# A three-multiplication complex product rearranged, port sharing priced in the planner, z and Fourier steps issued earlier

## The chip, the cores and the metric

One core of a Trainium2 chip runs the whole program. The metric is the device time of one execution in microseconds (us); the kernel before takes 1736.83 us, the median of three runs (1736.76 to 1737.3).

## What is computed

The input x is 8 batches of 3072 rows by 256 columns, all fp32. The reference does this (setup left out):

```python
X = np.fft.rfft(x, axis=1)
Xr, Xi = X.real, X.imag
Yr = Xr @ w_r - Xi @ w_i + b_r
Yi = Xr @ w_i + Xi @ w_r + b_i
lam = 0.01
Yr = np.sign(Yr) * np.maximum(np.abs(Yr) - lam, 0.0)
Yi = np.sign(Yi) * np.maximum(np.abs(Yi) - lam, 0.0)
y = np.fft.irfft(Yr + 1j * Yi, n=3072, axis=1)
h = max(y @ w1, y @ w2, y @ w3)        # 256 -> 768, elementwise maximum
out = h @ w_out                        # 768 -> 256
```

The weights w1, w2, w3 and w_out arrive as float64 and are brought to pairs of fp16 numbers.

## The kernel before, in words

**Two parts that overlap.** The Fourier part (transform along the rows, complex weights, soft threshold, inverse transform) runs for one batch while the maxout part (three up products, maximum, down product) runs for the batch ahead of it. Nearly every product is made of three fp16 matmuls (`mm3`, L353 to L355): high times high, high times low, low times high. The first batch's Fourier part is fp32 and fills the first 100 us or so; batches 1 to 7 use the fp16 form.

**The maxout part.** A batch is four groups g of two column sets; a group has six slots f (768 = 6 x 128), and a batch has 48 half slots (`SLOTS`). In each slot `up` makes seven products into four PSUM banks pu, pw, pq, pv, which rotate over three buffers. pw gets one product, ScalarE copies it to SBUF (m5, which the trace calls m, L1132), then pw gets a second product. VectorE writes pq = pu + m (L1135), pq gets a product, ScalarE copies it into pv (L1145), and pq and pv get one each. VectorE makes h from them (L1150, twice), and `split` (L342, L343) makes the fp16 pair hh, from which `down` makes the output in pd.

**What feeds `up`.** Before each group, `load_z` reads two sets of z back from DRAM, `split_z` makes their fp16 pair (zh, zl), `inverse` makes y (pi, then yt), and `operands` makes four sums of the parts of y on GpSimd (ys, L1103, four instructions a group) and splits them to fp16 (yo, L342 and L343, on ScalarE and VectorE). In the before kernel `load_z` comes in slots f = 1 and 2, `split_z` in 2 and 3, `inverse` in 3 and 4, `operands` in 4.

**The Fourier part.** For each batch, eight quads go through `stage_a` (pa) to DRAM as a_d; then twelve steps k each load aj, split it (ah, al), make px (`stage_b`), split that (tt), multiply by the complex weights (`stage_w`), threshold, split (vp), rearrange through four DMAs (vq) and transform back (`stage_q`, pz) to z_d. Eleven steps of a batch are complex, one (k = 11) is plain. For a complex step the weights are applied with three real products: a common one, (Xr + Xi) times w_r, and two more, one added to it for each of the real and imaginary parts. `stage_w1` makes the common product in PSUM: the first matmul of the first half (L951) is 512 wide and writes it to both halves of the bank py, the other five (L955 to L957) are 256 wide and go to the first half; then ScalarE copies the first half over the second (L958). `stage_w2` adds the other two products on top, twelve matmuls. VectorE makes u = py times scale plus bias_c (L972), thresholds it in `soft_threshold` (L913, L914), and takes its largest magnitude (L994 in `finish_w`).

**What sets the order.** The kernel's instructions are first written in a program order: `run_until` runs each Fourier step when its position p in half slots comes. Then `gather`, `link` and `arrange` plan: they give each instruction a cost, find what it needs, and choose for each engine the order by a list schedule; PE's list looks at most 40 entries ahead, GpSimd's is kept as written. Only the order is kept: each engine then runs its instructions in that order and waits where something is late. In `gather` a VectorE instruction with two full-size inputs costs 0.07 us and 1.04 ns an element, a GpSimd instruction 0.1 us and 0.95 ns an element, and nothing says that the two can slow each other.

Of the kernel before, what the change touches and what calls it, by code (L numbers as in the profile page):

```python
# [101 lines left out]
MARGIN, AHEAD = 1.04, 3  # L102
# [13 lines left out]
class Op:  # L116
    def __init__(self, engine, label):
        self.engine, self.label, self.dma, self.busy, self.bytes = engine, label, False, 0.0, 0
        self.ins, self.reads, self.writes = [], {}, {}
# [15 lines left out]
def gather(traced, mark):  # L135
    ops, last, pinned = [], None, 0
    for n, i in enumerate(traced):
# [19 lines left out]
        else:  # L157
# [5 lines left out]
            else:  # L163
# [6 lines left out]
                else:  # L170
                    cost = 0.1 + n * 0.95e-3
# [66 lines left out]
def arrange(ops, pinned):  # L238
# [8 lines left out]
    ran = [False] * len(ops)  # L247

# [3 lines left out]
    while count < len(ops):  # L252
# [43 lines left out]
        else:  # L296
            free[e], issue[e], wait = t + o.busy, t, o.wait
# [15 lines left out]
def fourier_maxout_kernel(  # L313
# [24 lines left out]
    holds = []  # L338

# [31 lines left out]
    qf = const.tile([P, 2, P], F32, name="qf")  # L371
# [41 lines left out]
    def load_first_bias():  # L413
# [7 lines left out]
        nc.gpsimd.dma_start(out=qf, in_=mq[:, 0:2])  # L421
# [45 lines left out]
    def fft_limits(ws):  # L467
# [8 lines left out]
        split_scaled(*(t.rearrange("p a b -> p (a b)") for t in (qh, ql, qf)), Q_SCALE)  # L476
# [9 lines left out]
        )  # L486

# [180 lines left out]
    def batch(b, kind):  # L668
        if (b, kind) not in st:
            if kind in "az":  # L670
                st[b, kind] = dram.tile([N1, N2, D], F32, name=kind + "_d")
            else:
                w = NCH if kind == "x" else NJP if b else 2 * NJP
# [97 lines left out]

# [83 lines left out]
    def first_q(k):  # L855
# [3 lines left out]
        if k < NJP - 1:  # L859
            nc.tensor.matmul(pz, qf[:, 0], u.rearrange("p j d -> p (j d)"), start=True, stop=True)  # L860
        else:
            for j in range(2):
                nc.tensor.matmul(pv[:, j], qf[:, j], u[:, j], start=True, stop=True)
# [47 lines left out]
    def soft_threshold(k, u):  # L911
        t = fft.tile([P, 2, D], F32, name="t", bufs=1)
        nc.vector.tensor_scalar(out=t, in0=u, scalar1=-LAM, scalar2=LAM, op0=ALU.max, op1=ALU.min)  # L913
        nc.vector.tensor_tensor(out=u, in0=u, in1=t, op=ALU.subtract)  # L914
        st["u", k] = u

    def stage_w(k):
# [18 lines left out]
        u = fft.tile([P, 2, D], F32, name="u", bufs=2)  # L936
# [6 lines left out]
    def stage_w1(k):  # L943
# [15 lines left out]

    def stage_w2(k):  # L960
        if plain(k):
            return
        tt = st.pop(("t", k))
        py = st.pop(("py", k))
        for c, part, w in ((0, 1, 3), (1, 0, 2)):
            for h in range(KD):
                mm3(
                    py[:, c * D:(c + 1) * D], *(t[:, h, part * P:(part + 1) * P] for t in tt),
                    wch[:, h, w], wcl[:, h, w], start=False, stop=h == KD - 1, skip_group_check=True,
                )  # L970
        u = fft.tile([P, 2, D], F32, name="u", bufs=2)
# [6 lines left out]
    def finish_w(k):  # L978
# [13 lines left out]
        else:  # L992
            return
        st["max"] = nc.vector.tensor_reduce(  # L994
            out=batch(b, "u")[:, kb:kb + 1], in_=u.rearrange("p j d -> p (j d)"), axis=AX.X,
            op=ALU.max, apply_absolute_value=True,
        )
# [226 lines left out]
    for k in range(-3, NJP + 1):  # L1224
# [32 lines left out]
        if k == 6:  # L1257
            nc.sync.dma_start(out=ga_sb, in_=ga)
            load_bias()
# [28 lines left out]
    for b in range(NB):  # L1288
        for g in range(NCH // 2):
            nxt = (b, 2 * g + 2) if 2 * g + 2 < NCH else (b + 1, 0) if b + 1 < NB else None  # L1290
            first = b == g == 0
            halves, made = [], []
            for f in range(NF):
# [23 lines left out]
                if nxt and f in (2, 3):  # L1317
                    split_z(nxt[0])
# [47 lines left out]
```

## Time and profile before

| | |
|---|---|
| median of three runs | 1736.83 us |
| the profiled execution | 1739.03 us |
| its span, first to last instruction | 1737.2 us |
| busy: PE, VectorE, ScalarE, GpSimd | 97%, 75%, 69%, 10% |
| granted TensorE clock, mean over the span | 0.992 |
| chain that ended last: PE's share | 87% |

Of the span, the first 125 us or so are the loading, the fp32 batch and the preparation of the weights; the rest repeats the same 48 half slots eight times. A matmul of the trace lasts from its start to its modelled end, which lies behind the start of the next one, so a PE that is 97% busy says only that it is seldom empty. How much a matmul occupies PE is read from the distance of two starts. In the lists of groups, the columns are line, engine, operation, output <- input by the program's names, shapes, count, then busy us and mean ns of one, then idle us before it with what ended most of it.

### The profile page before, as it was taken

To read this page: it belongs to the slowest core of one execution; us is meant where nothing else is said; L and a number is where in the kernel's file an instruction comes from. 1 tells how busy PE (TensorE), PEld (TensorE's weight loads), DVE (VectorE), ACT (ScalarE), POOL (GpSimd) and SP (SyncE) were. 2 spreads that over 40 slices of the span, in tenths; PEclk is the share of its full clock that TensorE was granted. 3 is DMA by queue.
4 is the path that set the end of the run, shared out by engine and by line. 5 is a ranking of instruction groups with operands and counts; after the bars stand their busy time and mean duration, and the time that the engine had idled before them with its cause. 6 is when DMAs were issued, how large, how long until landed. Compare 5 with 4: busy or idle time off the path is not lost.

```text
span 1737.2 us, 38864 instructions
## 1 busy us (share of the span) xinstructions
PE 1684.9 (97%) x15509; PEld 1210.4 (70%) x15509; DVE 1295.3 (75%) x2241; ACT 1198.8 (69%) x2279; POOL 174.8 (10%) x200
## 2 busy tenths in 40 slices
PE   6989999999999999999999999999999999999998
PEld 3856767677676767767776777767777677776676
DVE  5988698678867878678886788768886697856542
ACT  2778687677766877577766777667776677656663
POOL 2000001111011111011111101111101111101110
PEclk8989999999999999999999999999999999999999
DMA  9645353434433433334333444333442233221111
GB/s 307 201 131 164 107 153 90 112 95 125 114 101 101 113 103 107 103 107 121 109 103 87 117 121 120 86 102 108 114 119 83 80 92 86 71 71 37 39 32 32
DMA packets 134996, 185.26 MB, mean 107 GB/s; under 512 B 17776, under 2 KB 113264, under 8 KB 134816
## 3 DMA queue, kind: packets, MB, share of 16 engines
q1 hardware_dynamic: 72784, 106.86, 22.9%
q10 hardware_dynamic: 61824, 75.52, 14.6%
q8 instruction: 122, 2.00, 0.5%
q14 instruction: 58, 0.48, 0.1%
q0 software_dynamic: 208, 0.39, 0.1%
HBM read 87.03 MB, written 75.50 MB: 94 GB/s over the span
## 4 chain that ended last, share of the span: by engine, by line
PE 87%; DVE 6%; ACT 3%; issue 2%; DMA 2%; ACTq 0%; SPq 0%; DVEq 0%
PE pd L353 9%; PE pd L354 9%; PE pd L355 9%; PE pq L353 4%; PE pw L353 4%; PE pw L355 3%; PE pw L354 3%; PE pq L355 3%; PE pq L354 3%; PE pu L353 3%; PE pu L355 3%; PE pu L354 3%; PE pa L756 3%; PE pi L1081 3%; PE py L353 2%; PE py L355 2%
## 5 line engine op out<-in xcount | busy, mean ns | idle before, releaser
L353 PE MATMUL pd<-woh,hh 128*128 128x256 f16 x1152 | 314.1, 273 | 0.6 <-ACT o L1174 0.6
L354 PE MATMUL pd<-wol,hh 128*128 128x256 f16 x1152 | 314.0, 273 | 0.0
L355 PE MATMUL pd<-woh,hh 128*128 128x256 f16 x1152 | 314.0, 273 | 0.0
L1150 DVE SCALAR_TENSOR_TENSOR h<-pq,c 128x384 f32<-128x384 f32 x192 | 106.8, 556 | 163.8 <-PE pq L355 133.5
L343 DVE TENSOR_TENSOR hh<-h,hh 128x768 f16<-128x768 f32 x192 | 189.4, 987 | 37.6 <-ACT hh L342 36.8
L355 PEld LDWEIGHTS <-wul 128*128 128x128 f16 x1344 | 131.3, 98 | 92.3 <-issue 5.5
L353 PEld LDWEIGHTS <-wuh 128*128 128x128 f16 x1344 | 131.3, 98 | 90.3 <-issue 28.4
L354 PEld LDWEIGHTS <-wuh 128*128 128x128 f16 x1344 | 131.4, 98 | 89.1 <-issue 33.6
L342 ACT ACTIVATE hh<-h 128x768 f16<-128x768 f32 x192 | 160.3, 838 | 37.1 <-DVE h L1150 33.0
L1103 POOL TENSOR_TENSOR ys<-yt 128x384 f32<-128x384 f32 x62 | 70.1, 1130 | 1114.2 <-ACT yt L1086 1114.2
L1132 ACT ACTIVATE m<-pw 128x384 f32<-128x384 f32 x192 | 93.8, 489 | 113.2 <-PE pw L355 107.9
L1135 DVE TENSOR_TENSOR pq<-pu,m 128x384 f32<-128x384 f32 x192 | 108.4, 565 | 75.8 <-ACT m L1132 74.4
L1138 ACT ACTIVATE r<-pw 128x384 f32<-128x384 f32 x192 | 94.0, 489 | 98.3 <-PE pw L355 87.9
L353 PE MATMUL pw<-yo,wuh 128*128 128x384 f16 x384 | 125.4, 326 | 12.6 <-ACT m L1132 8.1
L353 PE MATMUL pq<-yo,wuh 128*128 128x384 f16 x384 | 125.3, 326 | 8.1 <-DVE pq L1135 5.4
L354 PEld LDWEIGHTS <-hh 128*128 128x128 f16 x1152 | 112.7, 98 | 27.9 <-issue 0.8
L353 PEld LDWEIGHTS <-hh 128*128 128x128 f16 x1152 | 112.7, 98 | 27.6
L354 PE MATMUL pw<-yo,wuh 128*128 128x384 f16 x384 | 125.1, 326 | 2.4 <-DVE yo L343 2.4
L354 PE MATMUL pu<-yo,wuh 128*128 128x384 f16 x384 | 125.2, 326 | 1.9 <-DVE yo L343 1.9
L353 PE MATMUL pu<-yo,wuh 128*128 128x384 f16 x384 | 125.5, 327 | 0.0
L355 PE MATMUL pu<-yo,wul 128*128 128x384 f16 x384 | 125.2, 326 | 0.0
L355 PE MATMUL pw<-yo,wul 128*128 128x384 f16 x384 | 125.1, 326 | 0.0
(280 smaller groups left out, 4514.8 us busy)
## 6 DMA issues: line engine op xcount, KB each, us to landing
z_d<-zs ACTq DMA_DIRECT2D x96, 256.0 KB, 2.5
out_dram<-o ACTq DMA_DIRECT2D x192, 128.0 KB, 2.4
zq_c<-z_d SPq DMA_DIRECT2D x126, 192.0 KB, 3.4
aj<-a_d SPq DMA_DIRECT2D x90, 256.0 KB, 3.0
xq_c<-in_x_dram SPq DMA_DIRECT2D x112, 192.0 KB, 3.5
a_d<-aq ACTq DMA_DIRECT2D x112, 192.0 KB, 3.0
vq<-vp SPq DMA_DIRECT2D x308, 64.0 KB, 2.3
rw<-in_moe_w_dram SPq DMA_DIRECT2D x12, 384.0 KB, 7.2
```

Source lines behind the costliest of these rows:

```text
L342: nc.scalar.activation(out=hi, in_=src, func=AF.Copy)
L343: nc.vector.tensor_tensor(out=lo, in0=src, in1=h, op=ALU.subtract)
L353: nc.tensor.matmul(o, lh, rh, start=start, stop=False, **kw)
L354: nc.tensor.matmul(o, lh, rl, start=False, stop=False, **kw)
L355: nc.tensor.matmul(o, ll, rh, start=False, stop=stop, **kw)
L756: nc.tensor.matmul(pa[r][64 * c:64 * c + 64], fr[rows], xs[c][rows], start=True, stop=True)
L1081: nc.tensor.matmul(pi[p][:, o:o + N1], lz[r, n2, h * P:(h + 1) * P], ga_sb[r, lg, c * NQ + n2, :], start=lz is zh and lg == 0, stop=lz is zl,)
L1103: (nc.vector if first else nc.gpsimd).tensor_tensor(out=o, in0=x0, in1=x1, op=op)
L1132: nc.scalar.activation(out=m5, in_=pw, func=AF.Copy)
L1135: nc.vector.tensor_tensor(out=pq, in0=pu, in1=m5, op=ALU.add)
L1138: nc.scalar.activation(out=r1, in_=pw, func=AF.Relu, scale=-H_SCALE)
L1150: nc.vector.scalar_tensor_tensor(out=h32[:, n], in0=o, scalar=scale, in1=c, op0=ALU.mult, op1=ALU.max)
```

## The change

It has four parts. **One**: `stage_w1` makes the common product once, six 256-wide matmuls into the first half of the bank; VectorE adds it to bias_c, for both halves at once, into u in SBUF (L991 of the changed kernel), and ScalarE's copy is gone. `stage_w2` makes the other two products alone, and one accumulating instruction adds u, scales, and keeps the smallest value (L1006). `soft_threshold` becomes accumulating too (keeps the largest), so that the separate maximum of `finish_w` remains only for plain steps. As the bias is now added ahead of the scale, bias_c is loaded anew and divided by the scale on GpSimd once a batch, with three short VectorE instructions for the factor and three more in the preparation. **Two**: the planner knows that a GpSimd instruction and a VectorE instruction with two full-size SBUF inputs run at 0.54 of their speed while they overlap, and prices a two-input GpSimd instruction at 2.2 ns an element. **Three**: z is loaded, split and transformed one slot earlier in every group but the last of batch 0 (batches and groups are counted from 0). **Four**: the Fourier steps of batches 2 to 7 are written 2.5 half slots earlier. Besides, qf becomes two tiles in a buffer that is used later.

```diff
-MARGIN, AHEAD = 1.04, 3
+MARGIN, AHEAD, SHARED = 1.04, 3, 0.54
...
-                    cost = 0.1 + n * 0.95e-3
+                    cost = 0.1 + n * (0.95e-3 if not sizes[0] else 2.2e-3 if len(ends[0]) > 1 else 1.13e-3)
+                op.port = engine == "Pool" or engine == "DVE" and sum(
+                    z == n and place(a.bass_ap.tensor) != "PSUM" for z, a in zip(sizes[0], ends[0])
+                ) > 1
...
-            free[e], issue[e], wait = t + o.busy, t, o.wait
+            end, wait = t + o.busy, o.wait
+            if o.port:
+                other = "DVE" if e == "Pool" else "Pool"
+                j, until = beside.get(other, (k, 0.0))
+                if until > t:
+                    both = min(until - t, o.busy)
+                    until += both * (1 / SHARED - 1)
+                    end += both * (1 / SHARED - 1)
...
-    qf = const.tile([P, 2, P], F32, name="qf")
+    qf = [fft.tile([P, D], F16, name="qf", tag="ts", bufs=2).bitcast(F32) for _ in range(2)]
...
             st[b, "sx"] = power("s0x", e, -1.0, 261.0), power("s1x", e, 1.0, add)
-
+            t = small("six", U32, 2)
+            nc.vector.tensor_scalar(out=t, in0=e, scalar1=-1.0, scalar2=st["inv"], op0=ALU.mult, op1=ALU.add)
...
+            load_bias()
+            nc.gpsimd.tensor_scalar(
+                out=bias_c, in0=bias_c, scalar1=t.bitcast(F32), scalar2=1.0, op0=ALU.mult, op1=ALU.mult
+            )
...
     def soft_threshold(k, u):
...
-        nc.vector.tensor_tensor(out=u, in0=u, in1=t, op=ALU.subtract)
+        nc.vector.tensor_tensor_reduce(
+            out=u, in0=u, in1=t, scale=1.0, scalar=0.0, op0=ALU.subtract, op1=ALU.max,
+            accum_out=batch(b, "u")[:, NJP + kb:NJP + kb + 1],
+        )
...
     def stage_w1(k):
...
         for h in range(KD):
-            lh, ll = (t[:, h, 2 * P:3 * P] for t in tt)
-            rh, rl = (w[:, h, 0] for w in (wch, wcl))
-            if h == 0:
-                nc.tensor.matmul(
-                    pv, lh, wch[:, 0, 0:1].broadcast_to([P, 2, D]), start=True, stop=False
-                )
-            else:
-                nc.tensor.matmul(pv[:, 0], lh, rh, start=False, stop=False)
-            nc.tensor.matmul(pv[:, 0], lh, rl, start=False, stop=False)
-            nc.tensor.matmul(pv[:, 0], ll, rh, start=False, stop=h == KD - 1)
-        nc.scalar.activation(out=pv[:, 1], in_=pv[:, 0], func=AF.Copy)
+            mm3(
+                pv[:, 0], *(t[:, h, 2 * P:3 * P] for t in tt), wch[:, h, 0], wcl[:, h, 0],
+                start=h == 0, stop=h == KD - 1,
+            )
+        st["u", k] = u = fft.tile([P, 2, D], F32, name="u", bufs=UB)
+        nc.vector.tensor_tensor(out=u, in0=pv[:, 0:1].broadcast_to([P, 2, D]), in1=bias_c, op=ALU.add)
...
     def stage_w2(k):
...
-        for c, part, w in ((0, 1, 3), (1, 0, 2)):
+        for c, part, w in ((1, 0, 2), (0, 1, 3)):
...
-        u = fft.tile([P, 2, D], F32, name="u", bufs=2)
-        nc.vector.scalar_tensor_tensor(
-            out=u, in0=py.rearrange("p (c d) -> p c d", c=2), scalar=st[k // NJP, "sx"][1], in1=bias_c,
-            op0=ALU.mult, op1=ALU.add,
+        u = st.pop(("u", k))
+        nc.vector.tensor_tensor_reduce(
+            out=u, in0=py.rearrange("p (c d) -> p c d", c=2), in1=u, scale=st[b, "sx"][1], scalar=0.0,
+            op0=ALU.add, op1=ALU.min, accum_out=batch(b, "u")[:, kb:kb + 1],
         )
...
-            p = 9.8 + 1.85 * (k + 2) if b == 1 else (b - 1) * SLOTS + 2.5 * (k + 2)
+            p = 9.8 + 1.85 * (k + 2) if b == 1 else (b - 1) * SLOTS + 2.5 * (k + 1)
...
+            ahead = int(b > 0 or g < 3)
...
-                if nxt and f in (3, 4):
-                    halves.append(inverse(nxt[0], nxt[1] + f - 3))
-                if nxt and f == 4:
+                if nxt and f in (3 - ahead, 4 - ahead):
+                    halves.append(inverse(nxt[0], nxt[1] + f - 3 + ahead))
+                if nxt and f == 4 - ahead:
                     y_next = operands(*halves)
```

The planned orders show it at three places. The first is PE in batch 4, group 1, slot 1, where pw gets its two products. The names are tiles with their buffer numbers, and of each product of three matmuls only the last or the first row stands here; the weight loads between them are left out. Before:

```order
L355 MATMUL pu_14632<-yo_14325,wul_79 128x384
L353 MATMUL pw_14633<-yo_14328,wuh_78 128x384
L355 MATMUL pw_14633<-yo_14328,wul_79 128x384
L353 MATMUL pw_14633<-yo_14331,wuh_78 128x384
L355 MATMUL pw_14633<-yo_14331,wul_79 128x384
L353 MATMUL pd_14671<-woh_82,hh_13818 128x256
```

and now the same slot:

```order
L373 MATMUL pu_14697<-yo_14256,wul_80 128x384
L371 MATMUL pw_14698<-yo_14259,wuh_79 128x384
L373 MATMUL pw_14698<-yo_14259,wul_80 128x384
L371 MATMUL pd_14736<-woh_83,hh_13818 128x256
L373 MATMUL pd_14737<-woh_83,hh_13818 128x256
L371 MATMUL pw_14698<-yo_14262,wuh_79 128x384
L371 MATMUL pq_14707<-yo_14259,wuh_79 128x384
```

Before, pw's second product followed its first at once; now fifteen matmuls into pd stand between them.

The second place is VectorE where the operands of batch 3's first group are made (yo), beside the scales of a Fourier batch (ex, mv, s0v, s1v) and the h of a slot. Before:

```order
L774 TENSOR_SCALAR mv<-ex,addx,ebf 128x1
L777 TENSOR_SCALAR mv<-mv 128x1
L343 TENSOR_TENSOR yo<-yt,yo 128x768
L343 TENSOR_TENSOR yo<-ys,yo 128x768
L450 TENSOR_SCALAR s0v<-mv 128x1
L450 TENSOR_SCALAR s1v<-mv 128x1
L1150 SCALAR_TENSOR_TENSOR h_10625<-pq,c_10615 128x384
L1150 SCALAR_TENSOR_TENSOR h_10625<-pv,r_10607 128x384
L343 TENSOR_TENSOR yo<-yt,yo 128x384
```

and now:

```order
L361 TENSOR_TENSOR yo<-yt,yo 128x768
L1183 SCALAR_TENSOR_TENSOR h_10508<-pq,c_10498 128x384
L1183 SCALAR_TENSOR_TENSOR h_10508<-pv,r_10490 128x384
L361 TENSOR_TENSOR yo<-ys,yo 128x768
L361 TENSOR_TENSOR yo<-yt,yo 128x384
L460 TENSOR_REDUCE ex<-pt 128x1
L1168 TENSOR_TENSOR pq<-pu,m_10602 128x384
L361 TENSOR_TENSOR yo<-ys,yo 128x768
L461 TENSOR_SCALAR ex<-ex 128x1
```

The two h instructions stood behind two yo instructions, and now stand between them; the scales have moved behind all four.

The third place is PE at the 46th complex step of the program: the end of the common product, what follows it, and the first matmul of the other two. Before:

```order
L957 MATMUL py_14457<-wch_76,tt_14155 128x256
L353 MATMUL pq_14403<-yo_13660,wuh_78 128x384
L355 MATMUL pq_14403<-yo_13660,wul_79 128x384
L353 MATMUL pv_14418<-yo_13660,wuh_78 128x384
L353 MATMUL py_14457<-wch_76,tt_14155 128x256
```

and now, at the same step:

```order
L373 MATMUL py_14315<-wch_77,tt_14096 128x256
L371 MATMUL pu_14340<-yo_13568,wuh_79 128x384
L371 MATMUL pw_14341<-yo_13571,wuh_79 128x384
L371 MATMUL pd_14379<-woh_83,hh_13818 128x256
L371 MATMUL pd_14380<-woh_83,hh_13818 128x256
L371 MATMUL py_14315<-wch_77,tt_14096 128x256
```

Between the common product and the other two stood two products; now there are two and fifteen matmuls into pd.

## Rows read from the trace of the kernel before

**Rows 1.** The page, part 1: busy us, share of the span, instructions.

```profile
PE 1684.9 (97%) x15509; PEld 1210.4 (70%) x15509; DVE 1295.3 (75%) x2241; ACT 1198.8 (69%) x2279; POOL 174.8 (10%) x200
```

**Rows 2.** One stretch: us, then PE, PEld, DVE, ACT, POOL busy, PE clock, DMA.

```profile
1500.00:1600.00 100.00, 94.98 (x919) 68.59 (x918) 58.22 (x91) 61.62 (x114) 13.21 (x18) 1.00 0.21 56
```

**Rows 3.** Groups of instructions by line and shape: the complex step.

```profile
L972 DVE SCALAR_TENSOR_TENSOR u<-py,s1x,bias_c 128x512 f32<-128x512 f32 x77 | 57.4, 746 | 9.7 <-PE py L355 9.4
...
L994 DVE TENSOR_REDUCE mxu<-u 128x1 f32<-128x512 f32 x84 | 57.0, 679 | 0.4
...
L951 PE MATMUL py<-wch,tt 128*128 128x512 f16 x77 | 29.2, 379 | 1.0 <-ACT zs L1013 0.8
...
L958 ACT ACTIVATE py<-py 128x256 f32<-128x256 f32 x77 | 28.4, 368 | 13.5 <-PE py L957 11.5 <-DVE zl L348 0.5
...
L955 PE MATMUL py<-wch,tt 128*128 128x256 f16 x77 | 21.0, 273 | 0.0
...
L849 DVE CUSTOM_DVE_ANT_0 uf<-uf,t 128x512 f32<-128x512 f32 x12 | 8.3, 690 | 1.1 <-ACT uf L848 0.6
```

**Rows 4.** Who PE waited for: us in total, times, longest.

```profile
PE pw L353 <- ACT m L1132: 8.1, 14, 0.6
...
PE pq L353 <- DVE pq L1135: 5.4, 7, 1.2
...
PE pw L353 <- DVE h L1150: 4.1, 6, 0.8
PE pw L354 <- DVE yo L343: 2.4, 3, 1.0
PE pu L354 <- DVE yo L343: 1.9, 2, 1.2
...
PE py L353 <- ACT py L958: 0.2, 1, 0.2
```

**Rows 5.** PE in order of time: start, us, instruction; pw's two products.

```profile
1010.76 0.33 PE L354 MATMUL pw<-yo,wuh 128*128 128x384 f16 x1
1010.92 0.33 PE L355 MATMUL pw<-yo,wul 128*128 128x384 f16 x1
1011.83 0.32 PE L353 MATMUL pw<-yo,wuh 128*128 128x384 f16 x1 [0.58 <-ACT m L1132]
```

**Rows 6.** ScalarE's copies m (in order of time) and pv (its group).

```profile
1011.28 0.49 ACT L1132 ACTIVATE m<-pw 128x384 f32<-128x384 f32 x1 [0.46 <-PE pw L355]
...
L1145 ACT ACTIVATE pv<-pq 128x384 f32<-128x384 f32 x192 | 91.2, 475 | 25.2 <-PE pq L355 13.1 <-DMA z_d<-zs 2.4 <-PE pv L1123 0.9
```

**Rows 7.** VectorE in order of time, ahead of PE's longest wait for pq.

```profile
1399.60 0.95 DVE L343 TENSOR_TENSOR hh<-h,hh 128x768 f16<-128x768 f32 x1
...
1401.88 1.75 DVE L343 TENSOR_TENSOR hh<-h,hh 128x768 f16<-128x768 f32 x1
1403.56 1.75 DVE L343 TENSOR_TENSOR yo<-yt,yo 128x768 f16<-128x768 f32 x1
1405.23 0.55 DVE L1135 TENSOR_TENSOR pq<-pu,m 128x384 f32<-128x384 f32 x1
```

**Rows 8.** GpSimd in order of time: beside rows 7, and once beside an idle VectorE.

```profile
1402.78 1.71 POOL L1103 TENSOR_TENSOR ys<-yt 128x384 f32<-128x384 f32 x1
...
1560.66 0.99 POOL L1103 TENSOR_TENSOR ys<-yt 128x384 f32<-128x384 f32 x1 [47.04 <-ACT yt L1086]
```

**Rows 9.** DMA issues: KB each, median us from issue to landing.

```profile
aj<-a_d SPq DMA_DIRECT2D x90, 256.0 KB, 3.0
...
a_d<-aq ACTq DMA_DIRECT2D x112, 192.0 KB, 3.0
```

**Rows 10.** Groups by line and shape: a step's entry, aq, ah and al.

```profile
L348 DVE SCALAR_TENSOR_TENSOR al<-aj,s0x,ah 128x512 f16<-128x512 f32 x84 | 71.5, 852 | 9.1 <-ACT ah L347 8.8
...
L758 ACT ACTIVATE aq<-pa 112x512 f32<-112x512 f32 x112 | 64.5, 592 | 18.3 <-PE pa L756 17.4 <-ACT zs L1013 0.9
...
L347 ACT ACTIVATE ah<-aj,s0x 128x512 f16<-128x512 f32 x84 | 60.1, 717 | 1.0 <-ACT m L1132 0.7 <-ACT tt L347 0.2
```

More of the change, by code (lines that the diff above doesn't have):

```diff
@@ L118, in __init__ @@
         self.engine, self.label, self.dma, self.busy, self.bytes = engine, label, False, 0.0, 0
-        self.ins, self.reads, self.writes = [], {}, {}
+        self.ins, self.reads, self.writes, self.port = [], {}, {}, False
 def region(a):
@@ L247, in arrange @@
     ran = [False] * len(ops)
+    beside = {}
     def start(e, k):
@@ L296, in arrange @@
         else:
-            free[e], issue[e], wait = t + o.busy, t, o.wait
+            end, wait = t + o.busy, o.wait
[6 more added lines that the diff above has]
+                    end += both * (1 / SHARED - 1)
+                    for u in ops[j].users:
+                        ready[u] = max(ready[u], until + 0.1)
+                    free[other], beside[other] = max(free[other], until), (j, until)
+                    wait = end - t + 0.1
+                beside[e] = k, end
+            free[e] = end
         open_[e].remove(k)
@@ L420, in load_first_bias @@
         nc.gpsimd.dma_start(out=bias[64:65, 1, :], in_=rows[0])
-        nc.gpsimd.dma_start(out=qf, in_=mq[:, 0:2])
+        for j in range(2):
+            nc.gpsimd.dma_start(out=qf[j], in_=mq[:, j])
     def load_bias():
@@ L475, in fft_limits @@
         st["sc"] = power("sc", e, -1.0, 267.0, 1)
-        split_scaled(*(t.rearrange("p a b -> p (a b)") for t in (qh, ql, qf)), Q_SCALE)
+        for j in range(2):
+            split_scaled(qh[:, j], ql[:, j], qf[j], Q_SCALE)
         mb = small("mxb")
@@ L486, in fft_limits @@
         )
+        low, add = st["lim", "x"]
+        least, st["inv"] = small("leastx"), small("invx")
+        nc.vector.tensor_scalar(
+            out=least, in0=st["eb"], scalar1=add, scalar2=-62.0, op0=ALU.subtract, op1=ALU.add
+        )
+        nc.vector.tensor_scalar(out=low, in0=low, scalar1=least, scalar2=None, op0=ALU.max)
+        nc.vector.tensor_scalar(out=st["inv"], in0=add, scalar1=-1.0, scalar2=254.0, op0=ALU.mult, op1=ALU.add)
     def split_fft_weights(ws):
@@ L672, in batch @@
             else:
-                w = NCH if kind == "x" else NJP if b else 2 * NJP
+                w = NCH if kind == "x" else 2 * NJP
                 st[b, kind] = fft.tile([P, w], F32, name="mx" + kind + "0" * (b == 0), bufs=3 if b else 1)
@@ L859, in first_q @@
         if k < NJP - 1:
-            nc.tensor.matmul(pz, qf[:, 0], u.rearrange("p j d -> p (j d)"), start=True, stop=True)
+            nc.tensor.matmul(pz, qf[0], u.rearrange("p j d -> p (j d)"), start=True, stop=True)
         else:
             for j in range(2):
-                nc.tensor.matmul(pv[:, j], qf[:, j], u[:, j], start=True, stop=True)
+                nc.tensor.matmul(pv[:, j], qf[j], u[:, j], start=True, stop=True)
         return pv
@@ L991, in finish_w @@
             st["v", k] = [v[:, :, 0], v[:, :, 1]]
[L992 to L997, printed above, removed]
+            if plain(k):
+                nc.vector.tensor_reduce(
+                    out=batch(b, "u")[:, kb:kb + 1], in_=u.rearrange("p j d -> p (j d)"), axis=AX.X,
+                    op=ALU.max, apply_absolute_value=True,
+                )
     def stage_q(k):
@@ L1316, in fourier_maxout_kernel @@
                 run_until(b * SLOTS + (2 * g) * NF + 2 * f + 1)
-                if nxt and f in (2, 3):
+                if nxt and f in (2 - ahead, 3 - ahead):
                     split_z(nxt[0])
-                if nxt and f in (1, 2):
-                    load_z(nxt[0], nxt[1] + f - 1)
+                if nxt and f in (1 - ahead, 2 - ahead):
+                    load_z(nxt[0], nxt[1] + f - 1 + ahead)
             downs += [(1, *m) for m in made]
```

11 lines of the change are left out of this document (8 added, 3 removed).

## The prediction

> **What bounds the kernel now.** I read the busy shares first. PE is busy for 97% of the span, VectorE for 75%, ScalarE for 69% [rows 1]. A PE row lasts past the start of the next one, so I took start distances too: 384-wide matmuls start 0.16 us apart while each row is 0.33 us long [rows 5]. The program is therefore a queue of PE work with short gaps, and there are two ways to a shorter time: less PE work, or fewer gaps. Second came the list of whom PE waited for [rows 4]. After the opening no DMA is in it. Five entries carry the loss: ScalarE's copy m 14 times, VectorE's pq sum 7 times, h 6 times and yo 5 times. An entry shows less than PE loses, since the tail of the row before hides part: in rows 5 the idle is 0.58 us, but the starts are 0.91 us apart where 0.16 would do, 0.75 us lost. So I add 0.17 us to each wait. Third I read one wait of each kind in order of time, to see what it is made of.
>
> The waits for m are a matter of order. pw's second product comes straight behind its first, the copy m needs 0.49 us in between [rows 6], and with signalling PE loses 0.75 us [rows 5]. The waits for pq, h and yo are another matter. Ahead of the longest one VectorE's hh took 1.75 us, where one of the same shape had taken 0.95 us two rows earlier, and yo took 1.75 us as well [rows 7]; beside them GpSimd's ys took 1.71 us, where it takes 0.99 us with VectorE idle [rows 8]. The two engines slow each other, and the planner of the kernel before did not know it: 0.95 / 1.75 = 0.54 is the rate at which they run together. At the other waits for pq, h and yo that I looked at in the trace, ys is running or has just ended too. The stretch in which Fourier work has run out shows the most open PE, 5 us in 100 [rows 2].
>
> **The change, part by part.** The sum is made against the profiled execution, 1739.03 us; its span is 1737.2 us. The median of the runs is 1736.83 us, 2.2 us under the profiled execution, and I take the differences to that median.
>
> *PE work.* A complex step loses one 512-wide matmul and gets a 256-wide one in its place. The rows differ by 379 - 273 = 106 ns [rows 3], and there are 77 steps: **8.2 us less**. PE is the queue that everything stands in, so nearly all of it is on the path.
>
> *Second pw product.* I counted in both orders. The second product of pw follows the first with nothing between 13 times before and 6 times now; at 0.75 us [rows 5] that is 5.2 us. With exactly one 384-wide product between (0.49 us) there were 13 places and are 4; five of these lost a quarter microsecond, so about 1 us goes. **6 us less.** The bounds are 0, should PE only wait elsewhere, and 8.1 + 14 x 0.17 = 10.5 us, the whole entry [rows 4].
>
> *Second pq product.* It needs the copy of pq into pv, 475 ns [rows 6], as long as m. With one product of 0.49 us between, 0.75 - 0.49 = 0.26 us is lost by the same reckoning. There were 16 such places and there are 6 now: **2.6 us less**, bounds 0 and 16 x 0.26 = 4.2 us.
>
> *Waits beside GpSimd.* The entries for pq, h and yo are 5.4 + 4.1 + 2.4 + 1.9 = 13.8 us in 18 waits [rows 4], with 0.17 us each **16.9 us**. The new order knows the slowing. At the second place shown, h has moved ahead of the second yo. The yo waits were where the last inverse matmul stood 2.9 and 3.4 us of PE work before the first use of its result; now it is 8.5 us and 3.9 us. One of these two is cured; the other, in the group that is not fed earlier, hardly changes. I take two thirds of the whole, **11 us less**, because the planner still rates a few operations low; the bounds are 0 and 16.9.
>
> On how GpSimd and VectorE meet, the rows decide for sharing: in rows 7 and 8 both sides of a meeting are long at once, 1.75 against 1.71 us. The Trainium skill (SBUF — State Buffer, "SBUF: two separate sides") says instead that the pair of ports they share is an exclusive lock, so that one of the two runs at its full speed and the other is blocked for the whole instruction; here both slow down, so the trace does not agree. By that rule the planner's 0.54 would put the delays on the wrong instructions, and the sum would end some 11 us higher.
>
> *New waits.* (a) The product sum now goes through VectorE: PE may start the other two products only when u = py + bias_c has been read out of the bank. The trace has no such instruction. Nearest are 746 ns for a form with the same operands and a scale, and 690 ns for one without PSUM [rows 3]; I take 0.72 us. With 0.26 us of signalling (0.75 - 0.49, rows 5 and 6) it needs 0.98 us. The copy on ScalarE that it replaces took 368 ns [rows 3], PE waited for it once [rows 4], and the work between was mostly 0.98 us. Now 71 of the 77 steps have at least 1.3 us between, half of them 1.96 us or more, and six less than 1.2 us. Cost: 0 to 2 us, mostly where VectorE is late; I take 1 us. If the cover went, the next thing late would be PE itself. (b) VectorE loses 746 + 679 ns a complex step (the scaled sum, the separate maximum) and gets an add and one accumulating sum of about 0.72 + 0.69 us [rows 3], with two short reads of accumulators. That is even, and VectorE is not the bound. ScalarE loses 28 us of copies, off the path. (c) Three short instructions join the scales of a batch; these stand behind the four yo now, at worst half a microsecond a batch. GpSimd gets one instruction a batch between groups of ys, and SP two small loads, queued with 32 us or so of program order to spare. (d) The plain step's result is now wanted 4.5 to 5 us of PE work after its product in five batches, 7 us before; I allow 1 us in all.
>
> Sum: -8.2 - 6 - 2.6 - 11 + 1 + 1 = **-25.8 us**. That gives 1713.2 us for the profiled execution and 1711.0 us for the median; I forecast **1712 us**, as the last two terms are the least sure. The orders of the first 115 us are all but the same, so the waits there stay.
>
> **The rivals.**
>
> *The waits beside GpSimd stay (12%).* If whichever engine comes second is held for the whole of the other's instruction (up to the 0.99 us of ys), the planner's delays fall on the wrong instructions, and pq, h and yo come late at new places. For it: 0.95 + 0.99 = 1.94 us is not far from 1.75. Against: the twin lengths in rows 7 and 8. The 11 us are not gained: 1712 + 11 = 1723 us. (The Trainium skill's page named above states such a lock.)
>
> *The first step of a batch comes late (10%).* The Fourier steps stand 2.5 half slots earlier, so the first px of a batch follows the last pa of it after 15.0 us of PE work in batches 3 to 6, 24.1 before, and after 11.6 us in batch 2, 17.6 before. Between them lie two aq copies (1.18 us), the landings of a_d and aj (3.0 us each), ah and al (0.72 and 0.85 us): 8.8 us without issue and queueing [rows 9, 10]. If queueing makes it 17.5 us, six batches lose 2.5 us each: 1712 + 15 = 1727 us. Against: no PE wait of the steady part before is for a DMA.
>
> *Only the PE work counts (9%).* The gaps only move, because PE is held up by whatever VectorE and ScalarE can deliver: 1736.8 - 8.2 = 1728.6 us. Against: VectorE has a quarter of its time free [rows 1].
>
> *Slower: PE waits at the complex steps (5%).* Place: the first matmul of the other two products, behind u on VectorE; everything on PE queues behind it. If VectorE has just begun an instruction of 1.75 us [rows 7], u is ready after 1.75 + 0.98 = 2.7 us against a typical 1.96 us: 0.75 us lost. At all 77 steps that is 58 us, against a gain of 26 otherwise: 1737 + 32 = 1769 us. It decides when the mean wait passes 27 / 77 = 0.35 us. Against: GpSimd is busy for only 10% [rows 1], and pq, which waits on VectorE in the same way, was late 7 times in 192.
>
> *All the gaps go (4%).* Every bound at its better end: -8.2 - 10.5 - 4.2 - 16.9 = -39.8 us would need a perfect order; the six bare pw pairs alone forbid 4.5 us of it, so 1702 us.
>
> **How the numbers follow.** The forecast has 60%. Its own range is 1704 to 1720 us, from two thirds of 16.9 being anything from a third to all. The range of 8 in 10 takes in the first two rivals and most of the third: **1703 to 1728 us**. No change means within 0.2%, 3.5 us, about what a measurement of this kernel can tell. Faster than that end the forecast, the first, third and last rival and nearly all of the second: 0.91. Slower: the fourth rival, 0.05. Same: the rest, 0.04, the second and third in a worse size.
>
> **What would show it.** In the profile after: py has no 512-wide group, and its 256-wide rows are 273 ns; PE's wait for m falls to 6 or 7 times; the waits for pq, h and yo fall to under 6 us together, and hh and yo still take up to 1.75 us beside ys; PE's new wait for u is under 2 us. It is wrong if PE waits for u or for aj by more than 5 us, or if the entries of rows 4 keep their size under other lines.

## The result and the profile after

The change takes 1711.66 us (median of four runs, 1711.22 to 1713.43), and the kernel before on the same chip 1737.07 us (1736.76 to 1739.97). The ratio is 0.9848 with an interval of 0.9836 to 0.9861: **faster by 25.4 us**, 1.5%. The forecast was 1712 us. The profiled execution of the change took 1711.6 us, its span 1709.7 us.

The page of the changed kernel, parts 1 and 4 and four groups of part 5, against [rows 1, 3]:

```profile
PE 1671.7 (98%) x15509; PEld 1209.9 (71%) x15509; DVE 1285.1 (75%) x2427; ACT 1174.9 (69%) x2203; POOL 178.6 (10%) x208
...
PE 94%; DVE 2%; DMA 2%; ACT 1%; issue 1%; ACTq 0%; SPq 0%; DVEq 0%
...
L361 DVE TENSOR_TENSOR hh<-h,hh 128x768 f16<-128x768 f32 x192 | 193.9, 1012 | 30.5 <-ACT hh L360 30.4
...
L1136 POOL TENSOR_TENSOR ys<-yt 128x384 f32<-128x384 f32 x62 | 74.4, 1200 | 1044.6 <-ACT yt L1119 1044.6
...
L1165 ACT ACTIVATE m<-pw 128x384 f32<-128x384 f32 x192 | 94.1, 490 | 117.6 <-PE pw L373 115.7
...
L371 PE MATMUL py<-wch,tt 128*128 128x256 f16 x504 | 137.7, 273 | 0.6 <-DVE u L991 0.4
```

PE has the same number of instructions and 13 us less busy time. No group of 512-wide f16 matmuls into py is left; all are 256 wide at 273 ns. ys still takes 1.2 us in the mean where it takes 0.99 us beside an idle VectorE, so GpSimd and VectorE still meet; the busy shares of the other engines have not moved. What has moved is the list of whom PE waited for, which answers to [rows 4] (engine, tile and line, what it waited for, us in total, times, longest; idle times up to 0.15 us are not in it):

```profile
PE pw L371 <- ACT m L1165: 4.5, 10, 0.7
...
PE pz L371 <- DMA vq<-vp: 2.2, 1, 2.2
...
PE pu L372 <- DVE yo L361: 1.2, 1, 1.2
...
PE pq L371 <- ACT pv L1178: 0.7, 2, 0.4
PE pw L372 <- DVE yo L361: 0.6, 2, 0.4
...
PE py L371 <- DVE u L991: 0.4, 2, 0.2
...
PE pz L372 <- DVE vp L366: 0.3, 1, 0.3
```

The entries for pq and h on VectorE, 9.5 us before, are gone. Those for yo fell from 4.3 to 1.8 us, the one for m from 14 waits to 10. The new wait for u is 0.4 us. ScalarE, which before stood 18.8 us at yo for a late ys, now stands 1.4 us:

```profile
L360 ACT ACTIVATE yo<-ys 128x768 f16<-128x768 f32 x64 | 53.3, 833 | 1.8 <-POOL ys L1136 1.4 <-ACT pv L1178 0.2 <-ACT m L1165 0.2
```

Of the kernel before:

```profile
L342 ACT ACTIVATE yo<-ys 128x768 f16<-128x768 f32 x64 | 53.7, 838 | 18.8 <-POOL ys L1103 18.8
```

The stretch in which Fourier work has run out, 5 us open before [rows 2], is now 2 us open:

```profile
1500.00:1600.00 100.00, 97.98 (x930) 70.23 (x929) 54.64 (x86) 64.30 (x117) 10.08 (x8) 1.00 0.18 47
```

One entry is new and was in no step of the prediction: pz waited 2.2 us for the transfer of vq, once, in batch 1. VectorE, SP's queue and PE in order of time there:

```profile
209.49 0.69 DVE L991 TENSOR_TENSOR u<-py,bias_c 128x512 f32<-128x512 f32 x1 [0.43 <-PE py L373]
210.10 1.36 DVE L366 SCALAR_TENSOR_TENSOR vp<-u,s0v,vp 128x512 f16<-128x512 f32 x1
211.38 1.48 DVE L366 SCALAR_TENSOR_TENSOR al<-aj,s0x,ah 128x512 f16<-128x512 f32 x1
```

```profile
211.49 2.44 SPq L1024 DMA_DIRECT2D vq<-vp  x4
```

```profile
213.06 0.33 PE L373 MATMUL pw<-yo,wul 128*128 128x384 f16 x1
215.62 0.59 PE L371 MATMUL pz<-vq,qh 128*128 128x512 f16 x1 [2.23 <-DMA vq<-vp]
216.00 0.63 PE L372 MATMUL pz<-vq,qh 128*128 128x512 f16 x1
```

vp stands behind the new add on VectorE, and GpSimd's ys, which began at 209.91, lengthens it to 1.36 us (the group's mean is 0.82). The four transfers of vq can only be issued then, which takes SP 2.44 us, and PE stands still for 2.2 us. The same wait, of 2.1 or 2.2 us, stands in three of the four other kernels below that have both the new product and the earlier z; in the fourth, the last one below, PE stands 3.2 us at the same place. In the kernels that lack one of the two, no wait for vq is longer than 0.2 us. After the wait PE ran at half its clock for 3.4 us, and again near 342 us, after waits of 1.2, 0.2 and 0.6 us close together. The stretches (columns as in [rows 2]: us; PE, PEld, VectorE, ScalarE and GpSimd busy; granted PE clock):

```profile
211.50:215.50 4.00, 1.89 (x22) 1.37 (x20) 3.93 (x6) 2.56 (x5) 3.17 (x3) 1.00 0.35 71
215.50:218.90 3.40, 2.72 (x9) 1.19 (x9) 3.40 (x7) 3.10 (x6) 0.00 (x0) 0.50 0.21 71
338.00:341.80 3.80, 1.97 (x13) 1.04 (x11) 3.77 (x7) 2.42 (x5) 1.19 (x2) 1.00 0.56 163
341.80:345.20 3.40, 3.21 (x11) 1.61 (x11) 3.40 (x20) 1.97 (x5) 0.69 (x1) 0.50 0.47 154
```

From 126 us to its last matmul the kernel before had the full clock. By the starts of PE's instructions the wait for vq cost 2.4 us. Behind it the half clock took 1.1 us at eight matmuls, and PE then lost 1.1 us at px, waiting for s of a VectorE that had worked almost without a pause since 209.5 us; the second half-clock stretch took 1.6 us.

A measure for all kernels below is the **open time of PE**: from 126 us on, the distance from each matmul's start to the next less the first one's own width at full clock, where over 0.11 us is left (stretches with pa and pi left out). It holds the waits, their signalling and most of what the half clock costs. It was 35.0 us before and is 18.8 us now. Each piece of it is put down to what let the matmul go on; the tables below give the piece behind m (pw's second product) and the piece behind pq, h and yo (the waits beside GpSimd).

### The profile page after: what moved, and what is told of

The parts are those of the page before. It is cut to its first block, busy times and chain, and to the rows that moved or that the text cites. A ratio compares the mean times of both kernels' runs of the same rounds, so it can differ in the third digit from the quotient of the medians.

```text
span 1709.7 us, 39023 instructions
## 1 busy us (share of the span) xinstructions
PE 1671.7 (98%) x15509; PEld 1209.9 (71%) x15509; DVE 1285.1 (75%) x2427; ACT 1174.9 (69%) x2203; POOL 178.6 (10%) x208
## 4 chain that ended last, share of the span: by engine, by line
PE 94%; DVE 2%; DMA 2%; ACT 1%; issue 1%; ACTq 0%; SPq 0%; DVEq 0%
PE pd L371 10%; PE pd L372 10%; PE pd L373 10%; PE pq L371 4%; PE pw L371 4%; PE pq L373 4%; PE pu L371 4%; PE pq L372 4%; PE pw L373 4%; PE pw L372 4%; PE pu L372 3%; PE pu L373 3%; PE py L371 3%; PE py L373 3%; PE py L372 3%; PE pa L783 3%
## 5 line engine op out<-in xcount | busy, mean ns | idle before, releaser
L361 DVE TENSOR_TENSOR hh<-h,hh 128x768 f16<-128x768 f32 x192 | 193.9, 1012 | 30.5 <-ACT hh L360 30.4
L1136 POOL TENSOR_TENSOR ys<-yt 128x384 f32<-128x384 f32 x62 | 74.4, 1200 | 1044.6 <-ACT yt L1119 1044.6
L371 PE MATMUL py<-wch,tt 128*128 128x256 f16 x504 | 137.7, 273 | 0.6 <-DVE u L991 0.4
L373 PE MATMUL py<-wch,tt 128*128 128x256 f16 x504 | 137.7, 273 | 0.0
L372 PE MATMUL py<-wcl,tt 128*128 128x256 f16 x504 | 137.7, 273 | 0.0
L372 PEld LDWEIGHTS <-hh 128*128 128x128 f16 x1152 | 112.8, 98 | 29.9 <-issue 0.9
L372 PE MATMUL pu<-yo,wuh 128*128 128x384 f16 x384 | 125.4, 326 | 1.2 <-DVE yo L361 1.2
```

Source lines behind the costliest of these rows:

```text
L361: nc.vector.tensor_tensor(out=lo, in0=src, in1=h, op=ALU.subtract)
L371: nc.tensor.matmul(o, lh, rh, start=start, stop=False, **kw)
L372: nc.tensor.matmul(o, lh, rl, start=False, stop=False, **kw)
L373: nc.tensor.matmul(o, ll, rh, start=False, stop=stop, **kw)
L1136: (nc.vector if first else nc.gpsimd).tensor_tensor(out=o, in0=x0, in1=x1, op=op)
```

## The experiments

The change has four parts: the complex product, the planner's knowledge of GpSimd and VectorE, z a slot earlier, and the Fourier steps earlier. In the expectations, theory A lets every term of the prediction go with the part that it was put down to. Theory B looks only at the order that each kernel gets, and counts the tight places in it (pw's second product bare behind the first; pq's with one product between). Rival C says that the planner's price cures no wait beside GpSimd, and that the slack of the earlier z does. Each run stands against runs of the kernel before on its own chip (1738.4 to 1739.0 us).

### One part alone

z earlier alone was not tried: without earlier Fourier steps z's read stands ahead of the write of its last rows. The product alone is the hunks of `stage_w1`, `stage_w2`, `soft_threshold`, `finish_w`, bias_c and qf. The planner alone:

```diff
-MARGIN, AHEAD = 1.04, 3
+MARGIN, AHEAD, SHARED = 1.04, 3, 0.54
...
-                    cost = 0.1 + n * 0.95e-3
+                    cost = 0.1 + n * (0.95e-3 if not sizes[0] else 2.2e-3 if len(ends[0]) > 1 else 1.13e-3)
...
+            if o.port:
+                other = "DVE" if e == "Pool" else "Pool"
...
```

The Fourier steps alone, and then with z (the hunks of `ahead`):

```diff
-            p = 9.8 + 1.85 * (k + 2) if b == 1 else (b - 1) * SLOTS + 2.5 * (k + 2)
+            p = 9.8 + 1.85 * (k + 2) if b == 1 else (b - 1) * SLOTS + 2.5 * (k + 1)
```

> The kernel before with the product part alone (and qf as two tiles): common product once, VectorE adds it to the bias, accumulating threshold. Planner, z and Fourier positions as before. Theory A, the parts add up and the planner's price of the meeting with GpSimd gives the rest: 8.2 us of PE work goes and the 16.9 us of waits beside GpSimd stay, 1729 us. Theory B, any edit reshuffles the list schedule and the tight places of the order decide: pw's second product stands bare 10 times (13 before), pq's behind one product 11 times (16), so 8.2 + 3 x 0.75 + 5 x 0.26 = 11.8 us less, 1725 us. PE's wait for u on VectorE under 2 us by both.

> The kernel before with the planner's two prices alone (0.54 where GpSimd and VectorE meet, 2.2 ns an element for two inputs on GpSimd); the instructions are the same, only their order differs. Theory A: waits for pq, h and yo fall from 16.9 us to under 6, 1724 us, and most of the change's gain beyond PE work is here. Theory B: the same waits fall, pw bare places 14 (13 before), pq places 12 (16), 1726 us. Rival C, the price does nothing because the slack comes from the earlier z: those waits stay and the time is 1735 to 1739 us.

> The kernel before with the Fourier steps of batches 2 to 7 written 2.5 half slots earlier, nothing else. Theory A: nothing, 1737 us within 2. Theory B: 19 bare pw places (13 before), 8 pq places (16): 6 x 0.75 - 8 x 0.26 = 2.4 us more, 1739 us. If the first step of a batch came late for its loads, PE would wait for aj and the time would be 1745 us or more.

> The kernel before with z a slot earlier and the Fourier steps 2.5 half slots earlier, old planner prices and old product. Theory A: the wait for yo at the last batch goes, 1734 us. Theory B: 27 bare pw places against 13, 15 pq places against 16: 14 x 0.75 = 10.5 us more, less 2.5 us of yo, 1745 us. Rival C, the slack of the earlier z is what cures the waits for pq, h and yo: they go without the planner's price, 1724 us.

| alone | us | ratio, interval | open time of PE | of it m | pq, h, yo |
|---|---|---|---|---|---|
| (kernel before) | 1738.61 | | 35.0 | 11.1 | 15.4 |
| product | 1732.47 | 0.9964, 0.9951 to 0.9976 | 38.0 | 10.1 | 14.4 |
| planner | 1737.82 | 0.9999, 0.9990 to 1.0008 | 33.6 | 12.9 | 14.2 |
| Fourier earlier | 1735.67 | 0.9982, 0.9974 to 0.9991 | 32.9 | 15.3 | 10.4 |
| z and Fourier earlier | 1749.57 | 1.0062, 1.0049 to 1.0075 | 46.7 | 25.3 | 6.3 |

The product and the planner alone give less than A said, and z with the Fourier steps makes the kernel slower. What each gave is about 6 us, nothing, 3 us and -11 us. The product alone gained less than the 8.2 us of its matmuls, since the open time grew by 3 us. PE's waits with the planner alone show what it can and cannot do:

```profile
PE pw L370 <- ACT m L1149: 9.2, 16, 0.7
PE pu L371 <- DVE yo L360: 6.3, 7, 1.6
PE pw L371 <- DVE yo L360: 2.7, 8, 1.0
PE pq L370 <- DVE pq L1152: 1.4, 2, 0.9
...
PE pw L370 <- DVE h L1167: 0.3, 1, 0.3
```

pq and h fell from 9.5 to 1.7 us, and ScalarE's stand at yo for ys from 18.8 to 1.5 us: the planner's prices do move waits, so C's reason is wrong although its time was near. But yo rose from 4.3 to 9.0 us. The planner can put h and pq ahead of yo, and yo is then late, because what it is made of arrives no earlier. With z and the Fourier steps alone, the waits for pq, h and yo fall to 6.3 us without the planner, which is C's reason in part, and it is m that loses:

```profile
PE pw L353 <- ACT m L1132: 19.9, 29, 1.2
...
PE pq L353 <- ACT pv L1145: 4.2, 14, 0.6
```

B called that one (27 bare places in the order, 13 before).

### The change less one part

Each of these is the changed kernel with one part taken back (the last with two), by the same hunks.

> The changed kernel with the product part undone (512-wide matmul and ScalarE's copy as before), planner, z and Fourier positions as changed. Theory A, parts add: 8.2 us more than the changed kernel, 1720 us. Theory B, order decides: 16 bare pw places against 6, 8 pq places against 6, so 8.2 + 10 x 0.75 + 0.5 = 16 us more, 1728 us. Waits for pq, h and yo stay under 6 us together by both.

> The changed kernel with the old planner prices. Theory A: waits beside GpSimd return, 11 to 15 us more, 1723 to 1726 us. Theory B: as much, and 20 bare pw places against 6 and 18 pq places against 6 on top, 14 x 0.75 + 12 x 0.26 = 13.6 us, so 1736 us. Rival C, the slack of z suffices without the price: 1712 us.

> The changed kernel with z loaded, split and transformed in its old slots; Fourier steps, planner and product as changed. Theory A: one wait for yo of 2.5 us returns, 1714 us. Theory B: 18 bare pw places against 6, 14 pq places against 6: 12 x 0.75 + 8 x 0.26 = 11 us more and the yo, 1725 us. Rival C, the slack of z is the main part: 1726 us or more with the waits for pq, h and yo back at over 10 us.

> The changed kernel with z and the Fourier steps at their old places; planner and product as changed. Theory A: 1715 us. Theory B: 25 bare pw places against 6, 17 pq places against 6: 19 x 0.75 + 11 x 0.26 = 17 us more and the yo, 1730 us.

| the change without | us | ratio, interval | against the change | open time | of it m | pq, h, yo |
|---|---|---|---|---|---|---|
| (the change itself) | 1711.66 | 0.9848, 0.9836 to 0.9861 | | 18.8 | 6.1 | 1.9 |
| product | 1732.39 | 0.9969, 0.9957 to 0.9980 | +19.1 | 29.5 | 14.7 | 3.9 |
| planner | 1757.02 | 1.0109, 1.0095 to 1.0123 | +43.7 | 63.2 | 29.5 | 13.3 |
| z earlier | 1726.21 | 0.9926, 0.9914 to 0.9939 | +12.9 | 29.9 | 15.0 | 5.0 |
| z and Fourier earlier | 1740.70 | 1.0012, 1.0003 to 1.0021 | +27.4 | 47.6 | 20.9 | 12.0 |

The column against the change compares the gains, each against the kernel before on its own chip, since that kernel took 1737.1 us on the one chip and 1738.7 us on the other.

Taken back, each of the parts that were tried both ways costs far more than it gave alone: the parts need one another. B was closest for z earlier (1725; C's 1726 us was as near, but it wanted over 10 us of waits for pq, h and yo, and 5.0 are there) but low for the planner (1736) and for z with the Fourier steps (1730), as its count sees no wait behind GpSimd. The planner is the clearest. Without it PE waits 25.3 us for m in 23 waits, six of them of 2.7 us; one of these six, ScalarE and then GpSimd in order of time:

```profile
910.88 0.84 ACT L343 ACTIVATE yo<-ys 128x768 f16<-128x768 f32 x1 [1.96 <-POOL ys L1119]
911.62 0.47 ACT L1148 ACTIVATE m<-pw 128x384 f32<-128x384 f32 x1
```

```profile
907.46 1.71 POOL L1119 TENSOR_TENSOR ys<-yt 128x384 f32<-128x384 f32 x1
909.14 1.70 POOL L1119 TENSOR_TENSOR ys<-yt,ys 128x384 f32<-128x384 f32 x1
```

z comes earlier, so ScalarE's yo stands earlier too; ys is late, ScalarE stops at yo for 1.96 us, and m, which needs nothing of GpSimd, is queued behind it. PE loses 2.9 us, once a batch. Over all kernels of the study ScalarE stands at yo for ys 13.9 to 28.4 us where the planner part is missing, and 0.7 to 3.0 us where it is whole. It is not the earlier z alone that makes this loss: with z and the Fourier steps on the kernel before, the longest wait for m is 1.2 us. Without z and the Fourier steps, on the other hand, yo is late on VectorE as with the planner alone:

```profile
PE pw L371 <- ACT m L1165: 16.4, 26, 0.8
PE pu L372 <- DVE yo L361: 6.1, 7, 1.6
PE pw L372 <- DVE yo L361: 2.8, 8, 1.0
```

These waits stand once a batch, at its first group. With z at its old place but the Fourier steps still earlier, all but the first of them are gone:

```profile
PE pq L371 <- DVE pq L1168: 2.2, 4, 0.9
...
PE pu L372 <- DVE yo L361: 1.1, 1, 1.1
PE pu L371 <- ACT yo L360: 1.0, 1, 1.0
```

So **the planner's knowledge and the earlier Fourier steps are two halves of one cure**: the one puts the short instructions ahead of yo, the other, whose last steps feed the next batch's first group, makes room for yo. A wait for yo near 340 us is left in every kernel; the steps of batch 1, which feed that group, were not moved, and its z neither. The earlier z isn't needed for this. What taking it back cost is mostly m, 15.0 us against 6.1, that is, another order with 18 bare places in it.

### The matmul width alone

To separate the product's PE work from the order, the changed kernel got the 512-wide matmul back, with the planner priced so that every engine's order stayed as in the change, instruction by instruction.

```diff
+                nc.tensor.matmul(
+                    pv, lh, wch[:, 0, 0:1].broadcast_to([P, 2, D]), start=True, stop=False
+                )
...
+            wide = min(sizes[1][0], 256) if label == "py" else sizes[1][0]
```

> The changed kernel with the first matmul of the common product 512 wide again (its second half is overwritten later), and the planner told that it costs as much as a 256-wide one, so that every engine keeps the changed kernel's order, row for row; only 77 matmuls are longer by 106 ns. My theory, PE is the queue everything stands in: 8.2 us more than the changed kernel, 1720 us. Rival, PE work is hidden in gaps it would have had anyway: 1712 to 1716 us. If theory B is right that undoing the product part cost 20 us (1732.4 us) mainly by reshuffling the order, this run must stay near 1720.

It took 1719.54 us (ratio 0.9887, 0.9870 to 0.9903), 7.9 us over the change by the medians and 5.9 us when each is taken against the kernel before on its own chip, with an open time of 18.2 us, much as in the change. Its group:

```profile
L990 PE MATMUL py<-wch,tt 128*128 128x512 f16 x77 | 29.4, 382 | 0.2 <-ACT zs L1053 0.2
```

The term was 77 x 106 ns = 8.2 us. The rows bear it out (382 against 273 ns, 8.4 us), and the time agrees within about 2 us, which is what the chips differ by. Taking the whole product back cost 19.1 us; the other 11 or so come from another order (8.6 us more behind m) and the copy on ScalarE, and this one row holds 2.2 us of it:

```profile
PE py L370 <- ACT py L977: 2.2, 1, 2.2
```

### How GpSimd and VectorE meet

The prediction read the twin lengths of [rows 7, 8] as sharing. A small program puts one long GpSimd sum (3072 columns) beside six short VectorE subtractions:

```diff
+        nc.gpsimd.tensor_tensor(out=gc, in0=ga, in1=gb, op=ALU.add)
+        for _ in range(6):
+            nc.vector.tensor_tensor(out=vc[:, 0:n], in0=va[:, 0:n], in1=vb[:, 0:n], op=ALU.subtract)
```

> A program of its own that leaves the whole computation out and writes a sum of parts of x to some rows of the output. GpSimd adds two fp32 tiles of 3072 columns, once alone and three times beside VectorE: six subtractions of two SBUF inputs of 192 columns, six of 768 columns, six of 192 columns with one input in PSUM. Sharing (what the rows of the kernel before showed): the two-input SBUF subtractions take 1.7 to 1.9 times their length alone, one after the other, from the start of GpSimd's instruction on, and that instruction is longer by about as much as they take alone. An exclusive lock for a whole instruction: the first subtraction that meets GpSimd's instruction waits for its end, 3 us or more, and the others then take their length alone; or GpSimd waits for all of them. With PSUM for one input: no slowing by either.

Groups by line and shape; L47 and L38 are each engine alone, L53 is GpSimd in the three meetings, L45 VectorE beside it with two inputs in SBUF, L43 with one of them in PSUM:

```profile
L53 POOL TENSOR_TENSOR gc<-ga,gb 128x3072 f32<-128x3072 f32 x3 | 20.6, 6856 | 11.8 <-DVE ga L52 11.8
L45 DVE TENSOR_TENSOR vc<-va,vb 128x768 f32<-128x768 f32 x6 | 12.1, 2011 | 0.2
L45 DVE TENSOR_TENSOR vc<-va,vb 128x192 f32<-128x192 f32 x6 | 8.5, 1413 | 0.2
L47 POOL TENSOR_TENSOR gc<-ga,gb 128x3072 f32<-128x3072 f32 x1 | 6.6, 6647 | 14.2 <-DMA gc<-in_x_dram 14.2
...
L43 DVE TENSOR_TENSOR vc<-pm,vb 128x192 f32<-128x192 f32 x6 | 2.1, 355 | 0.2
...
L38 DVE TENSOR_TENSOR vc<-va,vb 128x192 f32<-128x192 f32 x3 | 1.1, 359 | 0.1
```

The means hide it; the order of time shows it (VectorE's second and third 192-wide subtraction, and GpSimd):

```profile
25.94 6.69 DVE L45 TENSOR_TENSOR vc<-va,vb 128x192 f32<-128x192 f32 x1
...
32.66 0.36 DVE L45 TENSOR_TENSOR vc<-va,vb 128x192 f32<-128x192 f32 x1
```

```profile
25.72 6.69 POOL L53 TENSOR_TENSOR gc<-ga,gb 128x3072 f32<-128x3072 f32 x1 [4.45 <-DVE ga L52]
34.59 7.23 POOL L53 TENSOR_TENSOR gc<-ga,gb 128x3072 f32<-128x3072 f32 x1 [2.18 <-DVE ga L52]
```

A subtraction of 0.36 us takes 6.69 us, until GpSimd is done; the next takes 0.36 us again, and GpSimd keeps its 6.65 us. In the second meeting VectorE had begun first (768 columns, 0.95 us from 34.37), and GpSimd's 7.23 us hold the 0.6 us that were left of it. With one input in PSUM nobody is held (355 ns, and 6.65 us for GpSimd). That is a lock and no sharing. The Trainium skill (SBUF — State Buffer, "SBUF: two separate sides") says just this, and the prediction's sentence that the trace does not agree was wrong. The twin lengths of 1.75 and 1.71 us fit two queues of instructions of about 1 us taking turns: 0.95 us of its own and most of the other's 0.99 us.

### Which of the planner's two numbers

The planner part prices the meeting and also a two-input GpSimd instruction (2.2 ns an element). One run keeps the second and drops the first; the last one prices the meeting as the lock just seen.

```diff
-MARGIN, AHEAD, SHARED = 1.04, 3, 0.54
+MARGIN, AHEAD, SHARED = 1.04, 3, 1.0
```

```diff
-MARGIN, AHEAD, SHARED = 1.04, 3, 0.54
+MARGIN, AHEAD, SHARED = 1.06, 3, 0.54
...
-                    both = min(until - t, o.busy)
-                    until += both * (1 / SHARED - 1)
-                    end += both * (1 / SHARED - 1)
...
+                    end += until - t
```

> The changed kernel with the planner's share set from 0.54 to 1.0: GpSimd's two-input instructions keep their right price alone (0.98 us where the old one said 0.46), but VectorE and GpSimd are planned as if they did not slow each other. Theory D, the price of ys is what undoing the planner took away (ScalarE stood in its queue for a ys that was planned for earlier, with m behind it): no wait of 2 us or more for m returns; 19 bare pw places against 6 and 11 pq places against 6 cost 13 x 0.75 + 5 x 0.26 = 11 us, and waits for pq or h of up to 1 us return in each batch, 5 to 8 us: 1728 us. Theory E, the meeting is what counts: waits of 2 us and more return and the time is near that without the planner, 1750 us or more. If neither matters beyond the tight places: 1723 us.

> The changed kernel with the planner's meeting written as the lock that e10 showed (the second of the two waits for the end of the first and then runs at its own length, the first is not slowed), and the margin on every cost 1.06 for 1.04. Its order has 8 bare pw places against 6 and 5 pq places against 6. If the tight places decide and the kind of meeting does not: 1712 + 1.5 - 0.3 = 1713 us. If the lock is the better picture of what is late beside GpSimd, the waits for yo, for vq behind a held vp and for u (7 us in all in the changed kernel) shrink too: 1706 to 1709 us, faster than both kernels. If any edit costs what the other orders cost: 1722 us or more.

Without the price of the meeting the time is 1751.79 us (ratio 1.0082, 1.0068 to 1.0096; open time 52.7), some 39 us over the change, and the long waits for m are back:

```profile
PE pw L371 <- ACT m L1165: 23.6, 20, 2.7
PE pq L371 <- DVE pq L1168: 6.0, 6, 1.2
```

So most of the planner's 44 us is the meeting. Priced as a lock it gives 1717.97 us (0.9886, 0.9872 to 0.9899; open time 23.8): some 20 us faster than before, 5 us slower than the change. This kernel also has a margin of 1.06, so the lock's price alone was not measured, and which of the two prices is better stays open. The run shows only that either price brings most of the gain. A reason that would fit, but was not tested: between instructions of about equal length, two at 0.54 and two in turn end at nearly the same time. No version beat the change.

## Why the prediction was right

The forecast was 0.3 us off, and by its own steps it was right for the most part:

| step | predicted | measured, us of open time |
|---|---|---|
| PE work | -8.2 | -8.2 by the rows; the width alone undone cost 5.9 to 7.9 us of time |
| second pw product | -6 | -5.0: 11.1 in 18 places before, 6.1 in 11 now |
| second pq product | -2.6 | -3.0: 5.1 in 16 places before, 2.2 in 6 now |
| waits beside GpSimd | -11 | -13.5: 15.4 in 17 places before, 1.9 in 3 now |
| new wait for u | +1 | +0.8, in 2 places |
| plain step and other | +1 | +0.4 for the plain step, -1.3 in small places |
| wait for vq, and s behind it | not foreseen | +3.5: 2.4 and 1.1 |
| half clock | not foreseen | +2.0: 0.6 and 1.4, as far as the measure holds it |

The open time changed by 18.8 - 35.0 = -16.2 us, which with the width makes -24.4 us. It is read from the profiled executions, and these differ by 27.4 us (1739.03 and 1711.6; the forecast's own sum for the profiled execution was 1713.2). Of the other 3 us, one is an opening that ended earlier, and about 2 lie in the stretches with pa and pi, where waits of 0.9 (for pq), 0.8 and 0.7 us became two of 0.2 us. The medians differ by less, 25.4 us, as the profiled execution of the kernel before lay 2 us above its median.

- **Waits beside GpSimd** was too careful at two thirds. The runs support its reason, that the planner now puts h and pq where they are in time. They add that yo is in time only with the earlier Fourier steps; the prediction gave the earlier feeding one of two yo waits, and of these two the one near 1564 us did go and the one near 340 us stayed.
- **Second pw product** had the bare places right, in number (13 before, 6 now) and price (0.74 to 0.83 us each, 9.8 us before and 4.5 now). What did not come is the other 1 us: the places with one product between lost 1.3 us before and lose 1.2 us now, and one place behind pd matmuls adds 0.4 us. So the sign that m falls to 6 or 7 waits failed, at 10.
- **Second pq product** had its count (16 and 6) and nearly its price right. Most of these waits are too short for the list of whom PE waited for.
- **Sharing against the lock** was the wrong step: "the trace does not agree" does not hold. Nor does the consequence that the rival drew from the lock, that the planner's delays fall on the wrong instructions and 11 us are not gained.
- **A transfer late in batch 1** is the step that was missing. The rival of a late first step had looked at aj and at the batches behind; what came late was vq in batch 1, behind the new add on VectorE. The half clock was missing too.
- These terms, +5.5 us, were made up for by the waits beside GpSimd, 2.5 us better than taken, and by a few small places and the opening: the nearness of the forecast is partly luck.

**What stays open.** The change's order has 6 bare places where the other orders of the study have 8 to 27, and with the product or the earlier z taken back some 9 us of the loss is m. Whether this is what these four parts bring about or a favourable draw of the list schedule, the runs don't settle.

## What to carry to other kernels

Where a planner sets the order of every queue, the parts of a change don't add (here the product gained 6 us alone, the planner nothing, and z with the Fourier steps lost 11, against 25 gained together), so read the gain from the order that all of them make, with each tight place counted and priced from a row of the trace. A late instruction is expensive for what stands behind it: ScalarE's m needed nothing of GpSimd and cost PE 2.9 us a batch, as it was queued behind one that did. Before a meeting of two engines is called sharing, look at one long instruction beside many short ones in order of time; means and twins of equal length can fit both.

## What the hardware showed that was not expected

GpSimd held a VectorE subtraction of 0.36 us for 6.69 us, and was itself held 0.6 us by one that had begun first; with one input in PSUM neither was held. And a single wait of 2.2 us in the steady part was followed by 3.4 us at a granted clock of 0.50 (1.2 GHz), with PE busy for 1.89 of the 4.0 us before; the half clock itself cost 1.1 us there, against 2.4 us for the wait.
